# Two units' attention products in one cluster, and 17 pairs of token blocks by seven products

## The chip, the cores and the metric

One Trainium2 chip, one of its cores. The time is device microseconds for one execution of the whole program. Three runs of the kernel before gave 300.24, 300.67 and 301.27 us; the median is 300.67 us. The profile is a further execution, which took 301.17 us.

Five engines work side by side, each through its own queue in order: TensorE (PE, with its weight loads as PEld), VectorE (DVE), ScalarE (ACT), GpSimd (POOL) and SyncE (SP, which here only issues DMAs). An instruction that waits holds up everything behind it on its own engine.

## The reference, cut to what matters

Linear attention with a decay per head (retention), then a two-layer network with a tanh GELU. Eight batches, eight heads, 576 positions, head size 64:

```python
scores = scale * np.matmul(q, k.transpose(0, 1, 3, 2))
gamma = 1.0 - 2.0 ** (-5.0 - np.arange(H))
Dmat = np.where(rel >= 0, gamma[:, None, None] ** rel, 0.0)   # rel = i - j
ret = np.matmul(scores * Dmat, v)
x = ret.transpose(0, 2, 1, 3).reshape(8 * 576, 512)           # 4608 tokens
h = x @ w_in                                                  # 512 -> 2048
g = 0.5 * h * (1.0 + np.tanh(c * (h + 0.044715 * h ** 3)))
out = g @ w_out                                               # 2048 -> 512
```

## The kernel before

**Attention.** A batch's 576 positions are cut into five units: four of 128 positions and one of 64, so there are 40 units. The first four pairs of units (0 and 1, 2 and 3, 5 and 6, 7 and 8) go through "wide" code that the change leaves alone; the other 32 go one at a time. For a unit u the list of steps has: `L` (loads of q, k, v by SP), `q`, `k`, `v` (casts to fp16 with the decay, on DVE, ACT or POOL), `D` (transposes of q and k by a DMA on SP) or `t` and `y` (the same by PE and a copy), then `B,u,w` (`attend`), which is PE's part. `B` does four things: the product of unit w's queries with the running state (L498, 128 rows of the array), unit u's k-v products that go into the state (L516), unit u's scores (L526), and unit w's outputs from its masked scores (L536). The last three are 64x64 products, four to the array at once; between two groups of them PE does products on the whole 128x128 array. Behind `B`, DVE masks the scores (`m`, L651), adds the k-v products to the state (`a`, L667), and the state is copied to fp16 for the next units (`z`); ACT copies the outputs to `xT` (`x`, L555).

**Network.** The 4608 tokens are nine groups t of 512. `N,t,fc,half` is eight products of 128x256 for `h` (L708), `M,t,fc` four of 128x512 for the same amount of work; `F` and `G` are the GELUs behind them on ACT (L716). The second product, for two blocks of 128 tokens at a time (a "pair"), is done as seven half-size products in place of eight: `T` makes sums of blocks of `w_out` once (DVE, eight steps), `H` sums of blocks of g (DVE, four per pair), `W` the seven products (L809, eight instructions of 128x256 each), `V` the seven additions that assemble the result (L768 on DVE, or a copy by L241 on ACT). Fifteen pairs go this way. The four blocks of t = 0, and one block of t = 8, go by the plain product `O` (L734, four steps of four 128x512 instructions per block), and the last block by `P` (L857).

**PSUM.** There are eight banks. Two each go to `h` (pool `ps_h`), to the second product (`ps_o`), to the scores and states of `B` (`ps_s`) and to its outputs (`ps_x`). The two pools `ps_h` and `ps_o` each hand out one bank in turn; a step that takes a bank waits until the last reader of that bank has finished.

**Order.** The order of all work is one list, `ORDER`, at the head of the source. A loop at the end calls one function per step, and each step appends its instructions to its engines' queues. So the place of a step in the list sets the order on each queue, and nothing else moves it. `K` steps are products of the identity whose results nothing reads; they stand where PE waits for the first loads. SP's queue holds the loads, the DMA transposes and the stores `S` and `Q`; POOL's queue holds casts and the loads of the two weight matrices (`I`, `J`).

Of the kernel before, what the change touches and what calls it, by code (L numbers as in the profile page):

```python
# [12 lines left out]
F32 = mybir.dt.float32  # L13
F16 = mybir.dt.float16
# [3 lines left out]
Z,1,v Z,2,g L,0,0 L,0,2 q,0 L,0,1 k,0,a L,2,0 v,0,g g I,2,g I,1,g K,4 K,2 t,0,q,o K,4 K,2 X,0 a,0,1  # L18
y,0,q,a q,2 I,0,g Z,3,v t,0,k,h y,0,k,v I,3,g z,0,1,a L,2,1 a,1,1 k,2,g K,4 K,4 K,2 t,2,k,h o,1,1
Y,0,1 L,4,1 I,5,g Z,4,g m,0,1 t,2,q,o k,4,a K,4 Y,0,0 y,2,k,a y,2,q,a z,1,1,v m,0,0 K,4 R,0 t,4,k,o  # L20
Y,2,1 I,4,g L,2,2 c Z,0,g x,1 x,0 K,3 N,0,0,0 m,2,1 L,4,0 N,0,2,0 I,7,g y,4,k,v v,2,g L,5,0 F,0,0,0
I,6,g N,0,6,0 F,0,6,0 F,0,2,0 Z,5,v L,5,1 X,2 q,4 Y,2,0 K,1 t,4,q,o N,0,4,0 N,0,10,0 a,2,1 z,2,1,v
m,2,0 k,5,g F,0,4,0 N,0,8,0 J,1,g y,4,q,v a,3,1 q,5 L,5,2 F,0,10,0 R,2 J,0,g B,4,-1 z,3,1,v t,5,q,o
y,5,q,v L,7,0 x,3 N,0,12,0 F,0,8,0 x,2 J,2,g J,7,g F,0,12,0 m,4 N,0,14,0 L,4,2 J,3,g N,0,8,1 L,7,1
v,5,v F,0,14,0 F,0,8,1 t,5,k,o N,0,4,1 N,0,6,1 q,7 y,5,k,a Y,5,0 F,0,4,1 X,5 F,0,6,1 N,0,10,1 a,5,1
v,4,g t,7,q,o a,6,1 m,5,0 k,7,v J,5,g F,0,10,1 N,0,0,1 N,0,2,1 L,7,2 J,4,g F,0,0,1 y,7,q,a B,-1,4
Y,5,1 z,5,1,a N,0,12,1 t,7,k,o x,4 L,11,0 m,5,1 F,0,2,1 O,0,0 y,7,k,v J,6,g R,5 Y,7,0 O,0,4 x,5
m,7,0 L,9,0 M,1,0,0 F,0,12,1 v,7,v x,6 N,1,10,0 o,6,1 L,9,1 G,1,0,0 F,1,10,0 N,1,14,0 L,9,2 F,1,14,0
N,1,4,0 O,0,5 L,10,0 N,0,14,1 F,1,4,0 O,0,1 X,7 q,9 k,9,v T,3,1,v F,0,14,1 Y,7,1 O,0,2 N,1,8,0
F,1,8,0 N,1,12,0 O,0,6 O,0,3 M,1,0,1 e,0,0,v a,7,1 a,8,1 q,10 O,0,7 F,1,12,0 N,1,6,0 L,10,1 O,0,12  # L30
L,11,1 z,7,1,a m,7,1 O,0,13 e,0,1,a T,1,1,v D,9 O,0,8 z,8,1,g T,1,0,v G,1,0,1 F,1,6,0 z,6,1,g v,9,g
L,10,2 t,10,q,h R,7 L,12,1 y,10,q,v B,9,-1 O,0,9 T,3,0,v k,10,v m,9 x,7 t,10,k,h L,11,2 H,1,0,1,v
O,0,10 O,0,14 H,1,0,2,v L,12,2 v,10,g x,8 y,10,k,a q,11 M,1,0,2 T,2,0,v L,13,1 L,12,0 L,14,1 k,11,g
B,10,9 T,2,1,v k,12,g D,11 H,1,0,3,v N,1,6,1 a,10,0 a,10,1 G,1,0,2 v,11,g S,0,0 O,0,11 j,6,a F,1,6,1
L,19,1 m,10 N,1,12,1 T,4,0,v H,1,0,4,v F,1,12,1 k,13,g N,1,4,1 O,0,15 L,14,0 M,1,0,3 z,10,1,g
F,1,4,1 e,0,3,a q,12 x,9 T,4,1,v N,1,8,1 L,13,0 G,1,0,3 S,0,1 L,14,2 z,10,0,v j,3,a F,1,8,1 W,1,0,1
e,0,2,v L,17,1 v,14,g v,12,g B,11,10 W,1,0,6 m,11 D,12 L,15,0 V,1,0,0,a x,10 q,13 N,2,0,0 W,1,0,2
V,1,0,2,a a,11,0 D,13 V,1,0,1,v z,11,0,v a,11,1 N,1,14,1 F,2,0,0 W,1,0,7 F,1,14,1 i,0,g o,11,1
N,2,4,0 z,11,1,v B,12,11 a,12,0 N,2,8,0 m,12 F,2,4,0 k,14,v S,0,3 V,1,0,3,v z,12,0,g L,15,2 F,2,8,0
W,1,0,5 L,13,2 L,15,1 N,2,6,0 N,1,10,1 W,1,0,4 v,13,g F,2,6,0 i,1,g q,14 L,16,0 V,1,0,5,v N,2,10,0  # L40
F,1,10,1 L,16,2 N,2,2,0 L,17,0 F,2,10,0 W,1,1,1 x,11 a,12,1 V,1,0,4,v V,1,1,0,a B,13,12 W,1,0,3
L,16,1 a,13,0 q,16 q,15 V,1,0,6,v x,12 m,13 F,2,2,0 N,2,4,1 F,2,4,1 N,2,0,1 z,13,0,v F,2,0,1 a,13,1
N,2,2,1 k,15,v H,1,1,1,v H,1,1,2,v z,12,1,a k,16,v z,13,1,v M,2,12 W,1,1,2 F,2,2,1 M,2,13 v,15,g
W,1,1,6 L,19,0 D,14 D,15 H,2,0,3,v V,1,1,2,a G,2,12 B,14,13 G,2,13 N,2,8,1 H,1,1,3,v M,2,14 m,14
x,13 D,16 V,1,1,1,v L,18,1 B,15,14 F,2,8,1 H,1,1,4,v a,15,0 z,15,0,a W,1,1,7 N,2,6,1 m,15 L,18,2
x,14 a,15,1 v,16,g B,16,15 G,2,14 L,18,0 q,19 S,0,2 M,2,15 z,15,1,g V,1,1,3,v F,2,6,1 x,15 W,1,1,5
N,2,10,1 W,1,1,4 k,18,g a,16,0 a,16,1 G,2,15 F,2,10,1 H,2,0,1,v V,1,1,4,v k,17,g W,1,1,3 V,1,1,5,v
N,3,0,0 N,3,10,0 F,3,0,0 k,19,v q,18 W,2,0,1 z,16,0,g F,3,10,0 S,1,0 L,20,1 L,21,1 N,3,8,0 L,17,2
V,2,0,0,a k,20,v v,18,v D,18 N,3,4,0 o,16,1 q,17 F,3,8,0 D,17 V,1,1,6,v L,20,2 W,2,0,2 m,16
H,2,0,2,v N,3,6,0 F,3,4,0 H,2,0,4,v S,1,1 H,2,1,1,v L,23,2 L,21,0 D,19 L,24,1 L,24,0 W,2,0,6  # L50
z,16,1,g V,2,0,2,a v,17,v B,17,16 a,17,0 V,2,0,1,v z,17,0,g a,17,1 N,3,2,0 S,1,2 x,16 m,17 F,3,6,0
W,2,0,7 z,17,1,v B,18,17 x,17 L,20,0 H,2,1,3,v W,2,0,5 L,22,1 L,25,0 F,3,2,0 V,2,0,3,v m,18 a,18,0
L,21,2 N,3,14,0 z,18,0,a a,18,1 W,2,0,4 V,2,0,4,v F,3,14,0 V,2,0,5,v N,3,8,1 q,21 L,22,0 W,2,0,3
k,21,v H,2,1,2,v W,2,1,1 V,2,1,0,a F,3,8,1 B,19,18 V,2,0,6,v j,0,a N,3,4,1 W,2,1,2 W,2,1,6 V,2,1,2,a
N,3,0,1 W,2,1,7 F,3,4,1 F,3,0,1 V,2,1,1,v S,1,3 V,2,1,3,v S,2,0 L,26,0 L,19,2 q,22 q,20 N,3,14,1
D,20 H,2,1,4,v F,3,14,1 v,20,g z,18,1,v x,18 L,22,2 W,2,1,4 N,3,6,1 W,2,1,5 V,2,1,5,v F,3,6,1
N,3,12,0 D,21 W,3,0,1 V,3,0,0,a L,25,1 F,3,12,0 N,3,10,1 m,19 v,19,v L,23,1 B,20,19 V,2,1,4,v a,20,0
L,23,0 k,22,g N,3,12,1 L,29,0 L,27,0 H,3,0,1,v H,3,0,2,v W,3,0,2 F,3,12,1 F,3,10,1 W,2,1,3 k,24,g
m,20 N,3,2,1 V,3,0,2,a V,2,1,6,v v,21,g x,19 a,20,1 z,20,0,g N,4,0,0 F,3,2,1 H,3,0,4,v v,22,g
B,21,20 k,23,a N,4,6,0 D,22 F,4,0,0 W,3,0,6 q,24 k,25,v F,4,6,0 N,4,4,0 H,3,0,3,v V,3,0,1,v N,4,12,0  # L60
F,4,4,0 a,21,0 x,20 a,21,1 H,3,1,1,v v,23,v z,20,1,a o,21,1 m,21 W,3,0,5 W,3,0,7 z,21,0,a D,24
V,3,0,3,v S,2,1 F,4,12,0 N,4,2,0 B,22,21 F,4,2,0 q,23 V,3,0,4,v H,3,1,2,v x,21 W,3,0,4 q,25
V,3,0,5,v L,26,1 a,22,0 W,3,0,3 S,2,2 L,27,2 m,22 N,4,12,1 W,3,1,1 z,22,0,a D,23 L,24,2 F,4,12,1
V,3,0,6,v q,27 N,4,2,1 j,5,v L,26,2 N,4,0,1 F,4,2,1 a,22,1 z,21,1,g z,22,1,a L,25,2 B,23,22 L,28,0
V,3,1,0,a N,4,14,0 W,3,1,2 F,4,0,1 H,3,1,3,v N,4,4,1 W,3,1,6 F,4,14,0 V,3,1,1,v i,4,v S,2,3 F,4,4,1
m,23 x,22 V,3,1,2,a M,4,8 G,4,8 W,3,1,5 v,24,g L,28,1 v,25,g M,4,10 a,23,0 q,26 v,26,v G,4,10 L,27,1
N,4,14,1 W,3,1,7 a,23,1 V,3,1,3,v F,4,14,1 L,31,2 z,23,1,g M,4,9 z,23,0,a L,29,1 k,27,a B,24,23
H,3,1,4,v N,4,6,1 D,25 G,4,9 k,26,a L,29,2 M,4,11 x,23 L,28,2 W,3,1,4 F,4,6,1 V,3,1,4,v V,3,1,5,v
D,26 m,24 W,3,1,3 N,5,0,0 G,4,11 i,5,g V,3,1,6,v B,25,24 q,28 F,5,0,0 L,30,2 S,3,0 H,4,0,1,v W,4,0,1
k,28,v H,4,0,2,v x,24 S,3,3 V,4,0,0,a a,25,0 z,25,0,v N,5,2,0 W,4,0,2 F,5,2,0 m,25 N,5,6,0 D,27 D,28  # L70
a,25,1 B,26,25 N,5,14,0 H,4,0,4,v v,28,g S,3,1 L,30,0 v,27,v F,5,6,0 V,4,0,2,a N,5,8,0 x,25 F,5,14,0
W,4,0,6 H,4,0,3,v F,5,8,0 a,26,0 a,26,1 V,4,0,1,v v,29,g z,25,1,g L,32,0 N,5,10,0 z,26,0,v W,4,0,7
L,31,1 N,5,4,0 V,4,0,3,v H,4,1,1,v W,4,0,4 m,26 F,5,10,0 H,4,1,2,v B,27,26 x,26 W,4,0,5 L,32,2
V,4,0,5,v F,5,4,0 N,5,10,1 o,26,1 N,5,4,1 q,29 F,5,10,1 V,4,0,4,v m,27 W,4,1,1 V,4,1,0,a L,30,1
N,5,12,0 S,3,2 a,27,0 L,35,0 W,4,0,3 q,30 H,4,1,3,v V,4,0,6,v k,30,v H,4,1,4,v F,5,12,0 W,4,1,2
j,7,g W,4,1,6 F,5,4,1 z,26,1,a N,5,6,1 z,27,0,g k,29,g a,27,1 N,5,14,1 V,4,1,2,a H,5,0,1,v L,31,0
q,31 V,4,1,1,v L,36,2 D,30 W,4,1,7 V,4,1,3,v k,31,a B,28,27 F,5,6,1 F,5,14,1 a,28,0 W,4,1,5 S,4,1
H,5,0,2,v N,5,12,1 a,28,1 D,29 V,4,1,4,v z,28,0,a x,27 v,31,g z,28,1,v z,27,1,g N,5,0,1 F,5,12,1
W,4,1,4 L,34,0 N,5,8,1 L,33,1 F,5,8,1 m,28 F,5,0,1 B,29,28 m,29 v,30,g i,7,a V,4,1,5,v W,4,1,3
N,5,2,1 x,28 B,30,29 L,34,1 F,5,2,1 H,5,0,4,v x,29 a,30,0 V,4,1,6,v W,5,0,1 m,30 H,5,0,3,v V,5,0,0,a  # L80
H,5,1,3,v v,32,v a,30,1 S,4,0 N,6,0,0 z,30,0,g L,33,0 W,5,0,2 q,33 W,5,0,6 V,5,0,2,a N,6,12,0
V,5,0,1,v W,5,0,7 D,31 B,31,30 F,6,0,0 k,34,a L,34,2 x,30 q,32 V,5,0,3,v H,5,1,1,v W,5,0,5 M,6,8
L,36,0 q,34 a,31,0 L,32,1 k,33,v L,33,2 F,6,12,0 W,5,0,4 H,5,1,2,v G,6,8 N,6,2,0 i,6,a m,31
V,5,0,5,v F,6,2,0 M,6,9 q,35 W,5,1,1 G,6,9 M,6,4 G,6,4 L,35,1 V,5,0,4,v L,38,1 N,6,2,1 S,4,2 S,5,1
z,30,1,g k,32,v L,39,2 F,6,2,1 D,32 W,5,0,3 M,6,5 a,31,1 V,5,1,0,a z,31,0,a j,4,a G,6,5 W,5,1,2
V,5,0,6,v M,6,11 B,32,31 v,33,g o,31,1 V,5,1,2,a W,5,1,7 M,6,6 G,6,11 S,5,0 S,4,3 a,32,0 G,6,6 x,31
z,32,0,a D,33 W,5,1,6 m,32 v,34,g V,5,1,1,v M,6,7 M,6,10 a,32,1 z,31,1,v j,1,a V,5,1,3,v z,32,1,a
B,33,32 L,37,1 a,33,0 W,5,1,4 L,36,1 G,6,7 N,6,0,1 k,36,a G,6,10 k,35,g z,33,0,a F,6,0,1 L,37,0
# [856 lines left out]
```

## Time and profile before

| what | value |
|---|---|
| three runs | 300.24, 300.67, 301.27 us |
| profiled execution | 301.17 us, of which the span from first to last instruction is 299.1 us |
| TensorE's granted clock | 1.00 over the span |
| steps of PE in the list | 34 `B`, 124 `N`, 20 `M`, 105 `W`, 20 `O`, 12 `t`, 11 `K` |
| DMA | 49.51 MB, mean 166 GB/s |

The page gives busy time per engine, forty equal slices of the span in tenths, the chain of work that ended last, and groups of instructions by line. "Mean ns of one" of a matmul is its own length from start to end; matmuls overlap, so what one costs the kernel is the distance between two starts. That distance can be read from the chain, whose pieces give the time that a run of so many instructions took.

### The profile page before, as it was taken

The page shows a single profiled execution, that of the slowest core. Times are in us where ns is not written, and L with a number is a line of the kernel's source. Part 1 is how long each engine was busy: PE and PEld are TensorE (multiplying, and loading weights), DVE is VectorE, ACT ScalarE, POOL GpSimd, SP SyncE. Part 2 cuts the span into 40 slices and gives each one's busy share as a digit, 9 for nine tenths or more (in the row PEclk, how much of TensorE's full clock was granted, in tenths as well). Part 3 has the DMA queues.
Part 4 walks back from the last instruction along what each step waited for, and adds up shares of the span by engine and source line. Part 5 has one row for each costly group of instructions (what it writes and reads, how often), then busy time and mean ns, then how long its engine had stood idle before and what let it go on. Part 6 is the DMA issues. An engine that isn't in the chain of part 4 may idle for free.

```text
span 299.1 us, 9534 instructions
## 1 busy us (share of the span) xinstructions
PE 286.2 (96%) x4086; PEld 234.9 (79%) x4086; DVE 185.2 (62%) x408; ACT 144.5 (48%) x282; POOL 80.7 (27%) x125
## 2 busy tenths in 40 slices
PE   3898999999999999989999999999999999999995
PEld 1466777668887788878887888887788888888874
DVE  8566663599629687357835877777288274643310
ACT  2463663436346544335577445444584546433321
POOL 5980810391321312113121125134041130200000
PEclk9999999999999999999999999999999999999999
DMA  6999999937999987999997995897995507100303
GB/s 191 279 230 239 283 197 202 214 75 161 189 212 155 237 125 184 206 221 189 221 226 158 241 234 119 168 182 167 215 180 112 122 21 142 37 2 0 144 18 125
DMA packets 135370, 49.51 MB, mean 166 GB/s; under 512 B 117152, under 2 KB 129824, under 8 KB 135328
## 3 DMA queue, kind: packets, MB, share of 16 engines
q1 hardware_dynamic: 130976, 44.71, 67.8%
q0 software_dynamic: 4352, 4.20, 8.4%
q8 instruction: 32, 0.52, 0.8%
q14 instruction: 10, 0.08, 0.1%
HBM read 36.70 MB, written 9.44 MB: 154 GB/s over the span
## 4 chain that ended last, share of the span: by engine, by line
PE 79%; DMA 6%; POOL 6%; DVE 4%; SPq 2%; issue 1%; ACT 1%; ACTq 0%; POOLq 0%; DVEq 0%
PE hps L708 37%; PE ops L809 27%; PE ops L734 6%; DMA w_in_sb<-in_moe_w_in_dram 3%; PE sk L516 2%; PE x L498 2%; POOL w_in_sb L212 2%; DMA pages<-in_q_dram 2%; DMA pages<-in_v_dram 2%; PE sk L526 1%; POOL wide L407 1%; PE x L536 1%; SPq L189 1%; PE ops L857 1%; POOL v L392 1%
## 5 line engine op out<-in xcount | busy, mean ns | idle before, releaser
L708 PE MATMUL hps<-xT,w_in_sb 128*128 128x256 f16 (+2 forms) x1120 | 143.4, 276 | 1.5 <-DMA w_in_sb<-in_moe_w_in_dram 1.5
L716 ACT ACTIVATE gT<-hps 128x512 f16<-128x512 f32 x144 | 84.8, 597 | 79.3 <-PE hps L708 79.0
L708 PEld LDWEIGHTS <-w_in_sb 128*128 128x128 f16 x1120 | 105.4, 98 | 20.7 <-DMA w_in_sb<-in_moe_w_in_dram 2.5
L809 PEld LDWEIGHTS <-ssum 128*128 128x128 f16 x480 | 46.1, 98 | 7.4 <-issue 0.6
L809 PE MATMUL ops<-tsum,ssum 128*128 128x256 f16 x360 | 46.1, 273 | 0.0
L809 PEld LDWEIGHTS <-gT 128*128 128x128 f16 x360 | 34.6, 98 | 6.8 <-issue 1.5
L392 POOL TENSOR_TENSOR v<-pages,dec 128x512 f16<-128x512 f32 (+1 forms) x24 | 23.8, 1001 | 51.9 <-DMA pages<-in_v_dram 38.0
L768 DVE TENSOR_TENSOR ost<-u,ops 128x256 f32<-128x256 f32 x45 | 18.5, 417 | 27.0 <-PE ops L809 25.4
L809 PE MATMUL ops<-w_out_sb,gT 128*128 128x256 f16 x240 | 31.2, 273 | 1.4 <-DVE ost L768 1.4
L768 DVE TENSOR_TENSOR u<-u,ops 128x256 f32<-128x256 f32 x30 | 12.5, 418 | 29.6 <-PE ops L809 19.9
L243 POOL CAST sz<-s 64x256 f16<-64x256 f32 x26 | 14.7, 564 | 55.4 <-DVE s L667 37.9
L392 DVE TENSOR_TENSOR qk<-pages,dec 128x512 f16<-128x512 f32 (+1 forms) x32 | 22.1, 696 | 10.0 <-DMA pages<-in_q_dram 10.0
L768 DVE TENSOR_TENSOR ssum<-gT,ssum 128x1024 f16<-128x1024 f16 x30 | 22.7, 758 | 0.2
L768 DVE TENSOR_TENSOR ssum<-gT 128x1024 f16<-128x1024 f16 x30 | 21.8, 732 | 0.8 <-ACT gT L716 0.8
L555 ACT ACTIVATE xT<-x 128x512 f16<-128x512 f32 (+1 forms) x26 | 14.4, 563 | 13.8 <-PE x L536 13.7
L651 DVE TENSOR_TENSOR ret<-sk,mask 128x512 f16<-128x512 f32 (+1 forms) x32 | 19.8, 618 | 1.4 <-PE sk L526 1.4
L734 PE MATMUL ops<-w_out_sb,gT 128*128 128x512 f16 x80 | 19.6, 379 | 0.0
L241 ACT CAST sz<-s 64x256 f16<-64x256 f32 x36 | 14.5, 402 | 8.8 <-DVE s L667 6.8
L685 POOL TENSOR_TENSOR sz<-s,gend 64x256 f16<-64x256 f32 x8 | 7.7, 959 | 36.9 <-DVE s L667 22.6
L667 DVE TENSOR_TENSOR s<-s,sk 128x256 f32<-128x256 f32 x36 | 15.0, 416 | 4.2 <-PE sk L526 3.6
L241 ACT COPY ost<-ops 128x256 f32<-128x256 f32 (+2 forms) x20 | 7.9, 394 | 18.0 <-PE ops L809 9.9
L809 PE MATMUL ops<-w_out_sb,ssum 128*128 128x256 f16 x120 | 15.6, 273 | 0.5 <-DVE ost L768 0.5
(96 smaller groups left out, 273.5 us busy)
## 6 DMA issues: line engine op xcount, KB each, us to landing
out_dram<-ost SPq DMA_DIRECT2D x35, 256.0 KB, 3.2
pages<-in_q_dram SPq DMA_DIRECT2D x32, 256.0 KB, 5.0
pages<-in_k_dram SPq DMA_DIRECT2D x24, 256.0 KB, 4.8
pages<-in_v_dram SPq DMA_DIRECT2D x24, 256.0 KB, 4.4
pages<-in_v_dram SPq DMA_DIRECT2D x4, 512.0 KB, 7.5
pages<-in_k_dram SPq DMA_DIRECT2D x4, 512.0 KB, 6.9
w_in_sb<-in_moe_w_in_dram POOLq DMA_DIRECT2D x8, 256.0 KB, 10.0
w_out_sb<-in_moe_w_out_dram POOLq DMA_DIRECT2D x8, 256.0 KB, 10.6
```

The source lines that it names most:

```text
L241: nc.scalar.copy(out=o, in_=i)
L243: (nc.vector if eng == "v" else nc.gpsimd).tensor_copy(out=o, in_=i)
L392: eng.tensor_tensor(out=out, in0=s["raw"][:, i, 0:n], in1=dec[:, i // 2, s["j"], 0:n].unsqueeze(2).to_broadcast([128, n, D]), op=ALU.mult,)
L555: nc.scalar.activation(out=xT[:, :, o : o + G * (b - a)].rearrange("c p (h s) -> c p h s", s=G), in_=x[:, a:b].rearrange("c h p s -> c p h ...
L651: nc.vector.tensor_tensor(out=ret[:, :, 0:n], in0=now["sk"][:, :, 0, 0:n], in1=mask.unsqueeze(1).unsqueeze(1).to_broadcast([128, 2, n, G]) ...
L667: nc.vector.tensor_tensor(out=s32, in0=state[0], in1=kv, op=ALU.add)
L685: (nc.vector if eng == "v" else nc.gpsimd).tensor_tensor(out=z[o : o + 64, :, hl, :], in0=s32[o : o + 64], in1=gend[o : o + 64], op=ALU.mult,)
L708: nc.tensor.matmul(hps[:, i, :], w_in_sb[:, ct, 128 * (fc + i) : 128 * (fc + i) + 128], xT[:, ct, TB * t % XR + lo : TB * t % XR + hi], st ...
L716: nc.scalar.activation(out=gTs[t][:, fc : fc + TB // (hi - lo), lo:hi], in_=h.pop((t, fc, lo)), func=AF.Gelu_apprx_tanh, bias=0.0, scale=1.0,)
L734: nc.tensor.matmul(ops[t, tcc], gTs[t][:, ft, 128 * tcc : 128 * tcc + 128], w_out_sb[:, ft, :], start=(ft == 0), stop=(ft == NFC - 1),)
L768: (nc.vector if eng == "v" else nc.gpsimd).tensor_tensor(out=out, in0=a, in1=b, op=op)
L809: nc.tensor.matmul(p["ps", bank][:, HN * col : HN * col + HN], a[:, k], b[:, k], start=(k == 0 and i in (1, 6)), stop=(k == HK - 1), skip_ ...
```

## The change

The step `C,u,u2,w,w2,pool` is new. It calls `attend` with two units u and u2 for the k-v products and scores and two units w and w2 for the outputs. In PE's order: the products of w and of w2 with the state, then k-v products and scores of u, then those of u2, then the outputs of w and w2. The outputs of both lie in the two banks of `ps_x`. The scores and k-v products of u lie in `ps_s` as before; those of u2 take both banks of `pool`, which is `h` or `o`. For that the two pools become one tile of two banks each, handed out by `take`, in the same turn as before.

Of the 34 `B` steps 5 remain, and there are 15 `C` steps. Eleven of them name pool `h`, four name `o`.

The four blocks of t = 0 become two pairs, so 17 pairs go by seven products. `O` goes from 20 steps to 4, `W` and `V` from 105 to 119 each, `H` from 60 to 68. Of the eight `T` steps, which all stood before the first product of t = 1's first pair, six now stand before the first product of t = 0's first pair and two between its third and its last.

The list is made anew. `N` goes from 124 to 92 steps and `M` from 20 to 52 (4 of them in quarters in both); `t` and `y` go from 12 to 18 each and `D` from 30 to 27: q and k of units 9, 12, 21 and 24 are transposed by PE and unit 10's by a DMA. `K` steps go from 34 products to 39. Among the casts `k` moves from 9 on ACT, 12 on POOL, 15 on DVE to 12, 14, 10; `z` from 20, 20, 16 to 17, 23, 16; `V` has 85 steps on DVE in place of 75. At the start the first load is k of unit 0, then q of units 0 and 2, then v of 0 and 2; POOL's first weight load stands before the first cast of v; `w`, which makes ACT load its GELU table, is the second step and was the last. The last attention step `B,-1,39` stands earlier: more of the network's products come behind it.

```diff
-B,10,9 T,2,1,v k,12,g D,11 H,1,0,3,v N,1,6,1 a,10,0 a,10,1 ...
+z,10,0,a F,1,4,1 i,6,a F,1,6,0 B,9,-1 W,0,1,2 L,16,1 V,0,1,1,v m,9 L,15,0 L,13,0 C,11,12,9,10,h
...
+    banks = {
+        "h": ps_h.tile([128, 2, 512], F32, name="banks_h"),
+        "o": ps_o.tile([128, 2, 512], F32, name="banks_o"),
+    }
+    turn = {"h": 0, "o": 0}
+
+    def take(pool):
+        turn[pool] += 1
+        return banks[pool][:, turn[pool] % 2]
...
-    def attend(u, ux):
-        now, last = st.get(u), st.get(ux)
-        if last:
-            c, m = last["c"], last["np"]
-            x = ps_x.tile([128, 2, 2, HP, G], F32, tag="x", name="x")[:, :, 0]
-            last["x"] = x
-            first = {}
+    def attend(us, ws, pool=None):
+        us, ws = [u for u in us if u >= 0], [st[w] for w in ws if w >= 0]
+        if ws:
+            tile_x = ps_x.tile([128, 2, 2, HP, G], F32, tag="x", name="x")
+        first = {}
+        for e, last in enumerate(ws):
+            c, m, u = last["c"], last["np"], last["u"]
+            last["x"] = x = tile_x[:, :, e]
...
-        if now:
-            n = now["np"]
-            kT, qT = now["kT"], now["qT"]
-            sk = ps_s.tile([128, 2, 2, HP, G], F32, tag="s", name="sk")
+        for e, u in enumerate(us):
+            now = st[u]
+            n, kT, qT = now["np"], now["kT"], now["qT"]
+            if e:
+                take(pool), take(pool)
+                sk = banks[pool].rearrange("c i (a p s) -> c i a p s", a=2, p=HP)
+            else:
+                sk = ps_s.tile([128, 2, 2, HP, G], F32, tag="s", name="sk")
...
-        h[t, fc, lo] = hps = ps_h.tile([128, TB // n, n], F32, tag="h", name="hps")
+        h[t, fc, lo] = hps = take("h").rearrange("c (i n) -> c i n", n=n)
...
-            ops[t, tcc] = ps_o.tile([128, DM], F32, tag="o", name="ops")
+            ops[t, tcc] = take("o")
...
-        "B": lambda u, ux: attend(None if u < 0 else u, None if ux < 0 else ux),
+        "B": lambda u, w: attend([u], [w]),
+        "C": lambda u, u2, w, w2, pool: attend([u, u2], [w, w2], pool),
```

## The prediction

> **What bounds the kernel now.** I read the page's busy times first, then the slices, then the chain.
>
> ```profile
> span 299.1 us, 9534 instructions
> ...
> PE 286.2 (96%) x4086; PEld 234.9 (79%) x4086; DVE 185.2 (62%) x408; ACT 144.5 (48%) x282; POOL 80.7 (27%) x125
> ...
> PE   3898999999999999989999999999999999999995
> ...
> DVE  8566663599629687357835877777288274643310
> ...
> PE 79%; DMA 6%; POOL 6%; DVE 4%; SPq 2%; issue 1%; ACT 1%; ACTq 0%; POOLq 0%; DVEq 0%
> ```
>
> PE's slices are full from the fifth on. The other engines' shares of the chain lie mostly in the first 30 us and in a few stalls. So behind the start, the time is what PE issues plus what it waits. The waits of PE alone say how little that is:
>
> ```profile
> PE busy L873 <- DVE ident L338: 4.5, 1, 4.5
> PE ops L809 <- DVE ost L768: 1.8, 2, 1.4
> PE hps L708 <- DMA w_in_sb<-in_moe_w_in_dram: 1.5, 3, 0.7
> PE x L580 <- ACT wide L241: 0.7, 1, 0.7
> PE sk L516 <- POOL v L392: 0.4, 1, 0.4
> ```
>
> Only the second and fifth lie behind the start. The larger of the two waits for DVE (1.4 us, at 132.4) is a late load: DVE stood 1.81 us before a cast of q whose load had not landed, until 129.01, and the addition that frees the bank was queued behind it.
>
> Prices next. The chain in order of time gives what runs of products cost:
>
> ```profile
> 183.10 2.62 PE ops L809 x24
> 216.47 1.73 PE hps L708 x8
> 289.95 2.59 PE ops L734 x12
> ```
>
> A 128x256 product takes 2.62/24 = 0.109 us, a 128x512 one 1.73/8 = 0.216 (2.59/12 agrees). And the timeline of PE around one `B`:
>
> ```profile
> 152.17 0.40 PE L498 MATMUL x<-qkT,sz 128*128 128x64 f16 x8
> 152.50 0.32 PE L516 MATMUL sk<-v,qk 64*64 64x64 f16 x16
> 152.65 0.30 PE L526 MATMUL sk<-qkT 64*64 64x64 f16 x16
> 152.77 0.30 PE L536 MATMUL x<-ret,v 64*64 64x64 f16 x16
> 153.01 0.50 PE L708 MATMUL hps<-xT,w_in_sb 128*128 128x256 f16 x3
> ```
>
> Eight L498 products cover 0.40 us and one lasts 0.193 (its group's mean), so they start (0.40 - 0.193)/7 = 0.030 apart: eight are 0.24 us, but L516 starts 0.33 behind. Going into the 64x64 products costs 0.09. Sixteen of them take 0.12 to 0.15; the last sixteen take 0.24 to the next large product. Coming out costs 0.12. A cluster costs 0.21 us over its work.
>
> **The change part by part.**
>
> *Pairs.* Two pairs lose 2 x 32 products of 128x512 (13.8 us) and get 2 x 56 of 128x256 (12.2 us): -1.6 us on PE.
>
> *N to M.* 32 times, eight products of 0.109 (0.872) become four of 0.216 (0.864): -0.3.
>
> Against both stands a rule of the Trainium skill (TensorE: Matmul & The Clock Gate, Back-to-back issue gap): in a real stream a 512-wide product costs about 131 ns, and the 216 is that of an isolated one. Here whole streams keep 216, so the trace does not agree. By the rule these two parts together (64 more 512-wide, 144 fewer 256-wide) would give 64 x 0.131 - 15.7 = -7.3 in place of -1.9; that is a rival below.
>
> *Clusters.* 34 `B` become 5 `B` and 15 `C`. Some stand next to other 64x64 steps (`X`, `Y`, `R`) and share a cluster; counted along the two lists there are 43 clusters before and 31 after. 12 x 0.21 = -2.5.
>
> *Transposes.* Sixteen more by PE. Eight `tp` products take 0.45 us in the timeline (37.05 to 37.50): +0.9. DMA loses three transposes on SP's queue, which bounds nothing there.
>
> PE's own sum is -3.5 us.
>
> *The start.* Before, real work of the network begins at 20.29. v of unit 0 was the load behind q; now k and q of unit 2 stand before it too, 1 MB more. At the first 10 us' 227 GB/s it lands 4.6 us later, by 12.9 at worst in place of 8.3, and POOL's cast of it (1.9 us) also has two weight-load issues of 0.70 each (four took 2.79) before it. `X,0` moves from 10.6 to about 14.8; behind it two additions (0.42 each) and a mask (1.2) give 17.3, under the 18.4 that held `R,0` before. `t,5,q` however now stands ahead of `R,0`, and q of unit 5 is the seventh load: 3.7 MB with some 1 MB of `w_in` between, 20 us, and a cast of 1.2. (`g`, eight memsets or 1.3 us, moves ahead of the first cast of q on DVE; that ends at 8.5 and not 7.3, still under the fifteen `K` products that now stand before `t,0,q`.) `N` would begin at about 22.8 with 0.8 us more work already done: +1.7 at worst. At best the waits for `w_in` go (1.5, its first loads being issued earlier) and the GELU table's load (1.28 on ACT at 20.26, for which PE waited 0.2): -1.7. The five more `K` products, 1.1 us, fill waits of this stage. I take +0.2.
>
> *Sums of w_out.* Eight `T` of 0.78 come before t = 0's first pair. The last load of `w_out` was issued at 37.6 and takes 10.6 to land. POOL's work before that issue in the new list comes to some 25 us from 7.7 on, so 33 to 38; landed by 44 to 49. The third product, the first that needs them, stands 26.4 us of PE's work behind the first `N`, so at 47 to 49. Up to 2 us if both are at their bad ends; I take nothing, since the middle values (46.5 and 48) leave room for the two `T` in front of that product that read the last load.
>
> *Banks held.* No row of before shows this. `C` needs both banks of a pool: the last GELU of 0.6 has at least one step (0.87) and `C`'s own first part (0.8) to end in, so going in is free unless ACT is late. Coming out, the next `N` or `W` of that pool waits until DVE has read u2's scores and states. For each `C` I added DVE's steps in the list up to the last such read (a = 0.42, m = 0.68 or 0.42, H = 0.75, V = 0.42, z = 0.6, o = 0.44, k = 0.51) and PE's up to the next taker. `C,31,32`: DVE 5.0, PE 3.5. `C,11,12`: 4.4 against 3.5. `C,25,26`, `C,27,28`, `C,37,38`: 3.5 against 2.6. `C,33,34`, `C,35,36`, `C,17,18`: PE has the more. Eleven are short, by 6.8 us in all. That is the upper end, if DVE starts only when `C` ends. It need not: u's states are done 0.6 us before (u2's group and the outputs come behind them), which leaves 2.1, and `H` and `V` at the front of six need nothing of `C`. Below: 0. I take +0.8, near the lower end, because DVE has an idle share to run ahead in.
>
> *DVE and the loads.* DVE gets eight `H` (6.0), ten `V` (4.2), five `y` (2.1), one `v` (0.7), loses five `k` (2.6) and one `e` (0.7): +9.7 us. It lies beside PE's work:
>
> ```profile
> 40.00:130.00 90.00, 89.24 (x1308) 72.09 (x1307) 59.78 (x115) 43.18 (x85) 24.57 (x33) 1.00 0.91 183
> 130.00:230.00 100.00, 98.63 (x1512) 83.33 (x1511) 70.55 (x144) 54.76 (x112) 25.15 (x31) 1.00 0.89 188
> ```
>
> (Columns: stretch, length, busy PE, PEld, DVE, ACT, POOL, clock, DMA share, GB/s.) DVE is 66% and 71% busy there; with the 9.7, and with the last attention step 38.0 us of PE's work before the end where it stood 27.5, it comes to about 78%. DMA is at 0.90; the last load stands some 7 us of PE's work earlier, 0.93. Both still fit, and ACT (-0.3) and POOL (+4) do too. I take nothing here, and the same few stalls as before; if the cover is gone, each late load costs PE about 1.4 us, the row at 132.4.
>
> *Sum.* -1.6 - 0.3 - 2.5 + 0.9 + 0.2 + 0.8 = -2.5. The profiled execution took 301.17 us (2.07 around its span), which is 0.5 over the median of 300.67. It would take 298.7; on the median's scale 298.2.
>
> **Rivals.** 0.3%, 0.9 us, is about what a measurement of this kernel tells from no change.
>
> A, slower: the held banks become a wait of PE behind every short `C`, all 6.8 us of it: 300.67 - 3.5 + 0.2 + 6.8 = 304.2. It decides from a mean of (3.5 - 0.2)/15 = 0.22 us per `C`. For it: DVE is in order and busier. Against: DVE's idle shares, and the waits on DVE before were two. A page speaks for it: the Trainium skill (Perfetto Trace Analysis, Optimization Strategy) reads a gap that recurs on the engine that should be full as too little PSUM for the next tile; no row of before shows one.
>
> B, no change: late loads. A denser DVE and DMA turn two stalls of the 132.4 kind into four: +2.8, 301.0. For it: DMA share 0.90 to 0.93. Against: three fewer DMA transposes.
>
> C, more: the start's waits for `w_in` go and the holds cost nothing: 300.67 - 3.5 - 1.5 = 295.7.
>
> D, wide products that overlap more than 0.216 apart allows: with the rule's 131 ns, 300.67 - 7.3 - 2.5 + 0.9 + 0.2 + 0.8 = 292.8. Every stream in the chain speaks against it, so it gets no chance.
>
> **How the numbers follow.** Forecast 0.59 (own range 296.7 to 299.7), A 0.13, B 0.13, C 0.15, D 0. Faster 0.59 + 0.15 = 0.74, same 0.13, slower 0.13. The range goes from under C, 294.8, to 302.0, which takes in B and the beginning of A.
>
> **What would show it.** Clusters: the starts behind L516, L526 and L536 groups, 31 times about 0.21. Pairs: 952 products of L809, 16 of L734, at 0.109 and 0.216. Holds: PE waiting on DVE at L651 or L667 right behind a `C`; over 3 us in all makes me wrong. Start: the first L708 between 19 and 23 us. Loads: PE waiting on L768 behind a DVE cast that waited for a load.

## The result and the profile after

The changed kernel takes 380.50 us (median of four runs, 376.42 to 382.73); the kernel before, run beside it, takes 300.46. The ratio is 1.263, with a 95% interval from 1.251 to 1.275. The prediction said 298.2 us, within 294.8 to 302.0, and gave a slower kernel 13 chances in 100. It was wrong by 82 us and in its sign. The profiled execution took 382.73 us, with a span of 381.0. Ratios in this text are of mean times and leave out a run more than 1.5% above the fastest of its kernel, as the profiled one is here (its mean granted clock was 0.982; that of the fastest, 376.42 us, was 0.995).

From the page of the changed kernel, engines, slices and the share of the chain:

```profile
span 381.0 us, 9471 instructions
...
PE 302.8 (79%) x4027; PEld 230.7 (61%) x4027; DVE 194.2 (51%) x427; ACT 141.0 (37%) x280; POOL 79.4 (21%) x132
...
PE   5866867877788968778887779879788878988776
...
PE 54%; ACT 10%; DVE 4%; issue 3%; ACTq 0%; DVEq 0%
```

PE has fewer instructions than before (4027 for 4086), and its work by the number of products is about 1 us less. But hardly a slice is full now: 79% in place of 96%. The loss is not in one place; it is spread over the whole span. ACT, which was 1% of the chain, is 10%, although it is busy for 3.5 us less than before. So an engine that has little to do has come onto the path, because PE stops for it again and again. The waits of PE alone (engine, its tile and line, what it waited for, and then us in all, how often, the longest):

```profile
PE banks_h L726 <- ACT gT L734: 42.3, 53, 2.3
PE banks_o L829 <- DVE ost L786: 5.3, 9, 0.9
PE banks_o L829 <- DVE u L786: 4.9, 7, 1.5
PE banks_h L892 <- DVE ident L340: 4.5, 1, 4.5
PE banks_o L829 <- ACT ost L243: 2.4, 5, 0.6
```

L726 is `N` and `M`, L734 the GELU, L829 `W`, L786 the additions `V`. Before, the waits of PE had no row for a GELU. Now 53 wait, 0.8 us each. A wait is counted from the end of the last product; undisturbed, the next step begins 0.17 us before that end (its eight products are issued in 0.87 us, but end after 1.04). So the 53 cost about 53 x 0.97 = 51 us. One of them in the timeline of the changed kernel, with PE's and ACT's lines (start, length, and in brackets the idle time before and what ended it):

```profile
338.50 1.04 PE L726 MATMUL banks_h<-xT,w_in_sb 128*128 128x256 f16 x8
...
339.57 0.60 ACT L734 ACTIVATE gT<-banks_h 128x512 f16<-128x512 f32 x1 [1.15 <-PE banks_h L726]
...
340.22 1.03 PE L726 MATMUL banks_h<-xT,w_in_sb 128*128 128x256 f16 x8 [0.68 <-ACT gT L734]
...
341.09 1.04 PE L829 MATMUL banks_o<-w_out_sb,gT 128*128 128x256 f16 x8
```

These are `N,8,10,0` and `N,8,14,0`, which follow each other on PE. Eight products are issued in 0.87 us. The second step begins 1.72 us behind the first: when the first step's products have ended (1.04), ACT reads the bank (0.60), and only then does PE go on. The second step writes the other bank. It had no reason to wait for the reader of the first.

It works the other way too. A GELU that stands in the list behind the next step's products waits for these as well:

```profile
96.39 1.91 PE L726 MATMUL banks_h<-xT,w_in_sb 128*128 128x256 f16 x16 [0.69 <-ACT gT L734]
...
98.33 0.60 ACT L734 ACTIVATE gT<-banks_h 128x512 f16<-128x512 f32 x1 [2.00 <-PE banks_h L726]
...
98.98 1.03 PE L726 MATMUL banks_h<-xT,w_in_sb 128*128 128x256 f16 x8 [0.69 <-ACT gT L734]
```

The first row is two steps, `N,1,14,1` and `N,2,0,0`. The GELU is that of the first, whose products end at about 97.4; it starts when those of the second have ended (98.30). The list has 66 such GELUs. None of them starts before the later products have ended, and the median one starts 1.75 us behind its own; in `split`, the first experiment below, that is 0.04.

To see all of this loss, I laid every step of PE's list on the trace: the distance from its first product to the next step's first, less the number of its products times their spacing (0.109 us for a 128x256 product, 0.216 for a 128x512 one, 0.056 for a transpose, 0.030 for the products with the state, 0.0075 for a 64x64 one). What is left over is lost. Before that is 20.4 us in all, in the changed kernel 102.0. In front of `N` and `M` it grew from 6.0 to 55.5, in front of `W` from 6.5 to 27.7. The `C` steps are not where it is: what stands in front of them comes to 1.5 us, and the waits of PE have no row for DVE's reads of u2's scores and states in `banks_h` or `banks_o`. A part of the loss is a lower clock: the granted clock is 0.50 in four stretches of 3.4 us, from 63.3, 206.7, 309.1 and 360.3 us on. Estimated from these lengths, that is at most 6.8 of the 82 us.

### The profile page after: what moved, and what is told of

Its sections match the earlier page's. It is cut to its first block, busy times and chain, and to the rows that moved or that the text cites. A ratio compares the mean times of both kernels' runs of the same rounds, so it can differ in the third digit from the quotient of the medians.

```text
span 381.0 us, 9471 instructions
## 1 busy us (share of the span) xinstructions
PE 302.8 (79%) x4027; PEld 230.7 (61%) x4027; DVE 194.2 (51%) x427; ACT 141.0 (37%) x280; POOL 79.4 (21%) x132
## 4 chain that ended last, share of the span: by engine, by line
PE 54%; ACT 10%; DVE 4%; issue 3%; ACTq 0%; DVEq 0%
PE banks_h L726 25%; PE banks_o L829 23%; ACT gT L734 8%; DVE ost L786 2%; PE x L511 1%; PE banks_o L752 1%; DVE u L786 1%; ACT ost L243 1%; DVE s L685 1%; PE x L554 1%; PE sk L533 1%; ACT sz L243 1%; PE banks_h L876 1%; PE sk L543 0%; PE banks_o L876 0%
## 5 line engine op out<-in xcount | busy, mean ns | idle before, releaser
L726 PE MATMUL banks_h<-xT,w_in_sb 128*128 128x256 f16 (+2 forms) x992 | 146.7, 294 | 42.3 <-ACT gT L734 42.3
L726 PEld LDWEIGHTS <-w_in_sb 128*128 128x128 f16 x992 | 94.8, 99 | 76.9 <-issue 51.9
L734 ACT ACTIVATE gT<-banks_h 128x512 f16<-128x512 f32 x144 | 82.3, 597 | 152.4 <-PE banks_h L726 148.2
L829 PEld LDWEIGHTS <-ssum 128*128 128x128 f16 x544 | 52.8, 98 | 23.9 <-issue 11.8
L829 PE MATMUL banks_o<-tsum,ssum 128*128 128x256 f16 x408 | 53.0, 275 | 9.3 <-DVE u L786 3.7
L786 DVE TENSOR_TENSOR u<-u,banks_o 128x256 f32<-128x256 f32 x34 | 14.3, 419 | 71.0 <-PE banks_o L829 60.5
L786 DVE TENSOR_TENSOR ost<-u,banks_o 128x256 f32<-128x256 f32 x51 | 21.0, 419 | 54.8 <-PE banks_o L829 44.2
L829 PEld LDWEIGHTS <-gT 128*128 128x128 f16 x408 | 40.1, 100 | 14.2 <-issue 6.5
L829 PE MATMUL banks_o<-w_out_sb,gT 128*128 128x256 f16 x272 | 37.0, 281 | 3.4 <-DVE ost L786 2.8
L786 DVE TENSOR_TENSOR ssum<-gT 128x1024 f16<-128x1024 f16 x34 | 23.9, 707 | 14.5 <-ACT gT L734 14.4
L786 DVE TENSOR_TENSOR ssum<-gT,ssum 128x1024 f16<-128x1024 f16 x34 | 23.8, 699 | 0.2
L829 PE MATMUL banks_o<-tsum,gT 128*128 128x256 f16 x136 | 17.6, 272 | 1.6 <-DVE ost L786 0.9
L829 PE MATMUL banks_o<-w_out_sb,ssum 128*128 128x256 f16 x136 | 17.6, 273 | 1.5 <-DVE ost L786 1.0
L892 PE MATMUL banks_h<-ident 128*128 128x512 f16 x39 | 11.3, 442 | 6.3 <-DVE ident L340 4.5
```

The source lines that it names most:

```text
L726: nc.tensor.matmul(hps[:, i, :], w_in_sb[:, ct, 128 * (fc + i) : 128 * (fc + i) + 128], xT[:, ct, TB * t % XR + lo : TB * t % XR + hi], st ...
L734: nc.scalar.activation(out=gTs[t][:, fc : fc + TB // (hi - lo), lo:hi], in_=h.pop((t, fc, lo)), func=AF.Gelu_apprx_tanh, bias=0.0, scale=1.0,)
L786: (nc.vector if eng == "v" else nc.gpsimd).tensor_tensor(out=out, in0=a, in1=b, op=op)
L829: nc.tensor.matmul(p["ps", bank][:, HN * col : HN * col + HN], a[:, k], b[:, k], start=(k == 0 and i in (1, 6)), stop=(k == HK - 1), skip_ ...
L892: nc.tensor.matmul(t, ident, ident.unsqueeze(1).to_broadcast([128, 4, 128]), start=True, stop=True, skip_group_check=True,)
```

## The experiments

**Theory.** The two banks of `h`, and the two of `o`, were two tiles of a pool before and are one tile of two banks now. A step that takes one bank of such a tile waits for every reader of the tile that stands ahead of it in the list, whichever bank it reads; and a reader waits for every step that writes the tile ahead of it. The order in which the banks are handed out is the same, but the two no longer work as two buffers. **Rivals.** The list itself is bad (loads, order, a full DVE), or the `C` steps hold both banks for long, as the prediction's rival A had it.

**Each bank a tile of its own.** `split` undoes this one thing in the changed kernel. The list and the clusters stay as they are; only u2's mask becomes two instructions of DVE, one for each bank.

```diff
-    ps_h = ctx.enter_context(tc.tile_pool(name="ps_h", bufs=1, ...))
-    ps_o = ctx.enter_context(tc.tile_pool(name="ps_o", bufs=1, ...))
+    ps_h = ctx.enter_context(tc.tile_pool(name="ps_h", bufs=2, ...))
+    ps_o = ctx.enter_context(tc.tile_pool(name="ps_o", bufs=2, ...))
...
     def take(pool):
-        turn[pool] += 1
-        return banks[pool][:, turn[pool] % 2]
+        p = ps_h if pool == "h" else ps_o
+        return p.tile([128, 512], F32, tag=pool, name="bank_" + pool)
...
-                sk = banks[pool].rearrange("c i (a p s) -> c i a p s", a=2, p=HP)
+                sk = [take(pool).rearrange("c (a p s) -> c a p s", a=2, p=HP) for _ in range(2)]
...
```

> The changed kernel with one edit: each of the four banks of the pools h and o is a tile of its own again; u2's scores and states lie in two such tiles, so its mask is two DVE instructions of 0.42 us in place of one of 0.68. List and clusters stay. Theory 1 (a tile of two banks is waited for as one, so every N waits for the GELU just before it): the 0.85 us behind most N and M go, and the time falls from 380 to 295 to 301 us, 298 in the middle. Theory 2 (the new list or the held banks are what costs): it stays above 360. Theory 3 (both): between 310 and 350.

Measured: 300.21 us (299.02 to 304.14), ratio 0.9973 (0.9945 to 1.0001) to the kernel before at 301.44. From its page, and its waits of PE:

```profile
PE 284.0 (96%) x4027; PEld 228.0 (77%) x4027; DVE 201.3 (68%) x441; ACT 143.2 (48%) x280; POOL 80.7 (27%) x132
...
PE   3976999999999999999999999999999999999995
```

```profile
PE bank_h L893 <- DVE ident L340: 4.5, 1, 4.5
PE bank_o L469 <- ACT wide L243: 3.4, 2, 2.7
PE x L592 <- ACT xT L560: 1.0, 1, 1.0
PE bank_o L469 <- DVE qk L400: 0.6, 1, 0.6
PE bank_o L469 <- DVE ost L787: 0.6, 1, 0.6
```

Eighty microseconds come back with the same list, the same clusters and the same products. Every wait for a GELU is gone, and the slices behind the start are full. No wait of PE behind a `C` shows either. That settles both rivals: neither the list nor the holds of `C` is the cause.

**The same thing done to the kernel before.** Three kernels take the old list and the old `B` steps, and make only the pool of `h`, only that of `o`, or both into one tile of two banks.

```diff
-    ps_h = ctx.enter_context(tc.tile_pool(name="ps_h", bufs=2, ...))
+    ps_h = ctx.enter_context(tc.tile_pool(name="ps_h", bufs=1, ...))
...
+    banks["h"] = ps_h.tile([128, 2, 512], F32, name="banks_h")
...
-        h[t, fc, lo] = hps = ps_h.tile([128, TB // n, n], F32, tag="h", name="hps")
+        h[t, fc, lo] = hps = take("h").rearrange("c (i n) -> c i n", n=n)
...
```

> The kernel before, with its own list and its single B steps; only the two pools h and o become one tile of two banks each, handed out in the same turn. Theory 1: 350 to 385 us, since its list too has many N close behind each other. Theory 2: 300 to 302 us, nothing changes. Theory 3: 320 to 350.

> The kernel before, only pool h as one tile of two banks. Theory 1: some 55 waits of up to 0.85 us for a GELU, 335 to 350 us. Theory 2: 300 to 302 us.

> The kernel before, only pool o as one tile of two banks. Theory 1: W waits for additions of both banks; the changed kernel's waits of PE on DVE and ACT at the second product suggest 310 to 330 us. Theory 2: 300 to 302 us.

Measured, with the kernel before at 301.44 us:

| kernel | us | ratio, 95% |
|---|---|---|
| `one_tile_both` | 354.45 | 1.178 (1.174 to 1.181) |
| `one_tile_h` | 340.95 | 1.131 (1.129 to 1.134) |
| `one_tile_o` | 319.26 | 1.060 (1.057 to 1.063) |

The waits of PE that cost most in `one_tile_h`, and two rows of `one_tile_o`:

```profile
PE banks_h L718 <- ACT gT L726: 28.4, 45, 1.7
```

```profile
PE banks_o L819 <- DVE ost L778: 6.9, 10, 1.2
PE banks_o L819 <- DVE u L778: 2.7, 5, 0.9
```

So the slow-down needs nothing of the clusters, the pairs or the new list. The two pools alone cost 39.5 and 17.8 us; both together cost 53.0 and not 57.3, since some waits of the one hide in waits of the other: in front of `W`, the accounting by steps has 20.2 us with `o` alone and 16.3 with both.

**Which pool costs what in the changed kernel.** `split` with one of the two pools made one tile again:

```diff
+    both = ps_h.tile([128, 2, 512], F32, name="banks_h")
+    turn = [0]
...
     def take(pool):
-        p = ps_h if pool == "h" else ps_o
-        return p.tile([128, 512], F32, tag=pool, name="bank_" + pool)
+        if pool == "o":
+            return ps_o.tile([128, 512], F32, tag=pool, name="bank_" + pool)
+        turn[0] += 1
+        return both[:, turn[0] % 2]
```

> split, but the pool of N and M (h) is one tile of two banks again, as in the changed kernel; o's banks keep their own tiles. Theory (a step that takes one bank of the tile waits for the reader of the other): of the 83.6 us that the changed kernel loses over split in front of PE's steps, 52.3 stand before N and M: about 300.2 + 52 = 352, and PE waits on ACT's GELU in front of some 55 N and M. Rival (only u2's scores and states, which span both banks in that tile, hold the pool): 9 of 15 C take h, at most 2 us each: under 318.

> split, but the pool of W, O and t (o) is one tile of two banks again; h's banks keep their own tiles. Theory: 23.4 us before W, 1.3 before O and 1.5 before t are what the changed kernel loses there over split: about 300.2 + 26 = 326. Rival (u2's six holds of o alone): under 312. If the two parts, this run's and that with h, add to less than the 80 us of both, waits of the one pool hide in those of the other.

Measured: 351.80 us with `h` as one tile, 329.23 with `o`. Over `split` that is 51.6 and 29.0, together 80.6, where the changed kernel stands 80.3 over `split`. The waits of PE in `split_but_h`:

```profile
PE banks_h L732 <- ACT gT L740: 41.4, 53, 1.6
PE banks_h L898 <- DVE ident L340: 4.5, 1, 4.5
PE bank_o L474 <- DVE qk L405: 2.7, 2, 1.6
```

These are again 53 waits, as in the changed kernel. The accounting by steps had said 52 and 26. Of the 3 us that it missed for `o`, 1.2 are the wait for k of unit 5 at the start, 3.9 us long in that profile and 2.7 in `split`'s; behind it PE works for 5.6 us at a granted clock of 0.50, in `split` for 3.4, which by an estimate from these lengths is about 1 us more. (Of the fifteen `C`, eleven put u2 into `h` and three into `o`, and one has no u2; what was expected counted nine and six.)

**What a cluster costs.** `split` gains only 0.3% over the kernel before. Its parts can still be tested. `cluster_cut` puts the whole-array products of w2 between the 64x64 products of u and those of u2, so that each `C` goes into 64x64 products twice. The products are the same.

```diff
-        for e, last in enumerate(ws):
+        def older(e, last):
...
+        if ws:
+            older(0, ws[0])
         for e, u in enumerate(us):
...
+            if not e and len(ws) > 1:
+                older(1, ws[1])
```

> split with each C cut in two: the products of w2's old state, of 128 rows, stand between u's 64x64 products and u2's, not in front of both. Same products, 15 more changes into 64x64 products and out of them. If a change in and out costs the 0.21 us that the prediction read from one B (0.26 by split's own mean over 20 steps), 15 of them cost 3.1 to 3.9 us: 303.3 to 304.1. If what B's cost is something else (the short products' own issue, or the wait for the first operands), nothing: 300.2.

Measured: 304.36 us, ratio 1.0087 (1.0051 to 1.0123), against `split`'s 0.9973: 3.4 us more by the ratios, 4.2 by the medians, just over what was expected. But the times of either kernel spread over 4 to 5 us, so the price is better read from the traces. In its profile the `B` and `C` steps take 8.08 us more than their products, in `split`'s 5.16. The difference is 2.92 us for 15 changes, 0.195 us each; it lies in the `C` steps alone, and every one of the 15 grows, by 0.15 to 0.23 us. (The rest of this profile's 6.2 us over `split`'s span lies elsewhere: the wait for k of unit 5 at the start is 2.2 us longer in it, and one transpose at 64 us waits 1 us for a cast.) So the price of 0.21 us that the prediction read from one `B` is that of a change in and out.

**The start.** Where is the rest of `split`'s expected gain? Its accounting by steps shows it: PE has lost 10.5 us by 33 us, where the kernel before had lost 8.1, and its `K` products come on top (8.4 us for 7.3). PE's timeline of `split`:

```profile
27.77 0.82 PE L469 MATMUL bank_o<-ident,wide 128*128 128x128 f16 x8 [2.75 <-ACT wide L243]
28.38 1.06 PE L638 MATMUL x<-qkT,sz 128*128 128x128 f16 x8
29.37 1.07 PE L650 MATMUL x<-xT,wide 64*64 64x128 f16 x32
30.37 1.57 PE L727 MATMUL bank_h<-xT,w_in_sb 128*128 128x128 f16 x16
31.86 0.42 PE L609 MATMUL sk<-qkT 64*64 64x128 f16 x16
```

and its windows of 2 us (stretch, length, busy PE, PEld, DVE, ACT, POOL, granted clock, DMA share, GB/s):

```profile
26.00:28.00 2.00, 0.23 (x4) 0.24 (x5) 0.00 (x0) 1.33 (x2) 0.00 (x0) 1.00 1.18 223
28.00:30.00 2.00, 2.00 (x39) 1.80 (x40) 0.89 (x2) 0.69 (x2) 0.00 (x0) 0.51 1.15 309
30.00:32.00 2.00, 2.00 (x44) 1.73 (x36) 0.50 (x1) 0.03 (x1) 1.39 (x1) 0.64 1.13 294
```

`t,5,k` transposes k of unit 5. ACT casts it, and its 512 KB land late. PE stands 2.75 us; behind that its granted clock is 0.51 and 0.64 for four microseconds, and the same steps take longer than in the next kernel (the group L638 1.06 us in place of 0.61). `start_mended` lets ACT do three more GELUs before this cast and moves work of the network in front of `t,5,k`.

```diff
-y,5,q,a z,1,1,v t,4,k,o L,7,0 F,0,4,0 k,5,a Y,2,1 a,2,1 z,2,1,v N,0,0,0 I,4,g N,0,2,0 a,3,1 L,7,1
-t,5,k,o F,0,0,0 m,2,1 R,2 y,5,k,v y,4,k,v L,4,2 M,0,12,0 F,0,2,0 I,5,g q,4 Y,5,0 t,4,q,o G,0,12,0
...
+y,5,q,a z,1,1,v t,4,k,o L,7,0 F,0,4,0 Y,2,1 a,2,1 z,2,1,v N,0,0,0 I,4,g F,0,0,0 N,0,2,0 a,3,1 L,7,1
+m,2,1 y,4,k,v R,2 F,0,2,0 x,3 N,0,6,0 x,2 L,4,2 I,5,g F,0,6,0 k,5,a N,0,4,1 F,0,4,1 t,5,k,o y,5,k,v
+q,4 M,0,12,0 G,0,12,0 Y,5,0 t,4,q,o N,0,6,1 F,0,6,1 M,0,12,1 v,5,g q,7 J,1,g G,0,12,1 X,5 M,0,12,2
...
```

> The changed kernel with each bank a tile of its own, as in split, with one stretch of the list mended: k of unit 5, whose load lands last, is cast on ACT behind the GELUs of N,0,0,0 and N,0,2,0 and not in front of them; t,5,k and Y,5,0 come later, N,0,6,0, N,0,4,1 and N,0,6,1 earlier. Theory (the start is what eats the gain): in split's profile PE stands 2.75 us before t,5,k (25.0 to 27.8), and its granted clock is 0.51 and 0.64 in the four us behind it, which costs about 1.9 us more. With the stall gone both go: 3 to 4.5 us under split's 300.2, so 295.5 to 297.5, a ratio of 0.98 to 0.99 to the kernel before; first N stays at about 21.7. Rival (DMA sets the pace there, and the stall only moves to the next product that needs a late load): 299.5 to 300.5, with a wait of PE of over 2 us elsewhere before 45 us.

Measured: 299.60 us, ratio 0.9953 (0.9933 to 0.9973). The rival was nearer. In its waits of PE the stall has moved, as the rival said it would:

```profile
PE bank_o L469 <- DVE qk L400: 2.1, 1, 2.1
PE bank_o L469 <- ACT wide L243: 1.8, 2, 1.3
```

`t,4,q` now waits 2.1 us for the cast of q of unit 4, which comes by the next of the late loads, and the clock in this execution is 0.63 in the two microseconds behind it. `start_filled` therefore brings still more of the network forward, work that needs no load which is still on its way:

```diff
-q,4 M,0,12,0 G,0,12,0 Y,5,0 t,4,q,o N,0,6,1 F,0,6,1 M,0,12,1 ...
+... N,0,4,1 F,0,4,1 k,5,a N,0,0,1 F,0,0,1
+N,0,6,1 F,0,6,1 t,5,k,o y,5,k,v N,0,2,1 F,0,2,1 q,4 M,0,12,0 G,0,12,0 Y,5,0 M,0,12,1 G,0,12,1 t,4,q,o
...
```

> start_mended, with the work of the network that needs no late load brought forward: N,0,6,0, N,0,4,1, N,0,0,1, N,0,6,1 and N,0,2,1 and two M stand in front of t,4,q, four of these N in front of t,5,k; N,0,0,1 and N,0,2,1 leave later places for it. If PE only ran out of work while the loads of units 4 and 5 were on their way, its waits between 20 and 38 us, about 5 us in start_mended's profile (1.0, 0.2, 0.5, 2.05 and some 1.2 at a granted clock of 0.63), fall under 2 and the clock stays at 1.00: 296.5 to 298, a ratio of 0.985 to 0.990. If the loads set the end of the whole start and not only of these steps, the wait comes back at a later load (X,5, t,7,q) and the time stays at 299 to 300.

Measured: 298.84 us, against 300.57 for the kernel before on the same chip: ratio 0.9934 (0.9912 to 0.9957). PE's timeline has these groups with an idle time before them from 20 to 38 us:

```profile
20.00 0.62 PE L470 MATMUL bank_h<-ident,wide 128*128 128x128 f16 x8 [0.38 <-DVE wide L416]
...
22.61 0.45 PE L593 MATMUL x<-wide,wide 64*64 64x64 f16 x32 [0.97 <-ACT xT L561]
...
28.55 2.78 PE L728 MATMUL bank_h<-xT,w_in_sb 128*128 128x256 f16 x24 [0.21 <-ACT xT L561]
...
36.99 0.42 PE L610 MATMUL sk<-qkT 64*64 64x128 f16 x16 [0.53 <-DVE xT L618]
```

Both long stalls are gone, and the clock is 1.00 in every window from 20 to 38 us. The time is 0.8 us over the upper end of what was expected: the gain at the start comes back as shorter losses later (the longest 0.9 us at 42 and 0.8 at 53, not far from where the two steps that were moved forward had stood). In this profile PE's last product ends at 294.2 us, in `split`'s at 294.1; but that execution of `split` (299.06 us) was among its shortest, and this one (299.36) among the longest of `start_filled`. So the traces show that the stalls are gone, and the gain itself rests on the times alone. By these, this is the version that beats both kernels, by 0.7% and some 21%.

## Why the prediction was wrong, step by step

**The step that failed is one that the prediction does not have.** It goes through pairs, clusters, transposes, start, sums, holds and loads, but the line of the diff that makes each of the two pools one tile of two banks is in none of them. I took it to be a renaming ("handed out by `take`, in the same turn as before") and so costed it at nothing without naming what covers it. The part that comes closest, *Banks held* (+0.8, with ends 0 and 6.8), asks only who waits behind a `C`. It should have asked who waits for whom in all 144 `N` and `M` and all 119 `W`, now that both banks have one name. The runs put +80 us there: 51.6 for `h` and 29.0 for `o`.

It could have been priced from what was known, if roughly. Eight products last 1.04 us, a GELU 0.60; in one buffer the next step can begin 1.72 us behind the last, not 0.87, which costs 0.85. Along the new list, 77 of the 144 `N` and `M` have the GELU of the `N` or `M` just before them ahead of them in the list, and in 24 of these no other work of PE lies between. Work that lies between can cover the wait. So the estimate runs from 24 x 0.85 = 20 us to 77 x 0.85 = 65 us, where 51.6 was measured. It is wide, and it leaves out the GELUs that wait for later products, but even its lower end would have turned the forecast from faster to slower.

**Rival A.** Its time (304.2) and its place (behind the short `C`, for DVE) were wrong. `split` has not one wait behind a `C`, although it holds the same banks for u2. What the prediction cited beside it fits the changed kernel better than its own use of it: the Trainium skill (Perfetto Trace Analysis, Optimization Strategy) reads the same gap, repeated on the engine that should be full, as too little PSUM for the next tile. The trace has the repeated gap, 53 waits of 0.8 us, but not for want of banks: there were as many as before, and two banks that are waited for as one are one buffer.

**The rest of the sum** can be judged in `split`, which has all of the change but the merged tiles. By steps on the trace:

| term | forecast, us | in `split`, us |
|---|---|---|
| pairs, `N` to `M`, transposes: PE's products | -1.0 | -1.0 |
| clusters | -2.5 | -3.05 |
| the start with its `K` products | +0.2 | +3.4 |
| holds and stalls behind the start | +0.8 | -1.4 |
| sum | -2.5 | -2.05 |

The sum is PE's last end, 294.1 us for 296.1; the profiled execution took 299.06 us for 301.17, and the medians differ by 1.2. The count of L809's products is as foretold, 952 (the page has them as 544 and 408, by their weights), and so are their spacings.

*Clusters*: the price was right, 0.195 by `cluster_cut`.

*The start* was mis-sized. I looked at what moves the first `N` and gave it +1.7 at worst; it did begin 1.4 us later (21.66 for 20.29 us), between the 19 and 23 us that I had named. I did not look behind the first `N`, at the loads of unit 5 that now come before the network has enough work, and I did not see that a stall there also lowers the clock.

*Sums of w_out*: no wait of a `W` for a `T` shows in `split`. *Holds*: none. *DVE and the loads*: DVE's busy time grew by 16 us and not 9.7 (the mask of u2 takes two instructions in `split`, which is part of it), and it stays hidden at 68%. One stall of the kind that I had read at 132.4 is left (0.7 us at 123, before `t,21,q`).

So had the banks kept their own tiles, the change would be worth 0.3% as its list stands (the interval includes 1.0), and 0.7% with the start put in order.

## What to carry to other kernels

What makes two buffers out of two banks is not the banks, but that they are waited for separately: before two buffers are put into one tile so that one instruction can reach both, ask of every user of either, all along the list, which reader of the other stands ahead of it, and of every reader, which later writer does; price the first at the reader's time plus the 0.17 us or so by which the last product's end lies behind the next one's turn. When a diff is costed part by part, a line that only renames or re-allocates is a part as well, and its price is zero only if the waits it makes are the same. And when work is moved in front of late loads, look behind the first product of the main work too: a stall of 2 to 3 us there can cost half as much again in clock (1.5 us behind 2.75 in `split`).

## What the runs showed of the hardware that I had not expected

**Idle time lowers the clock for microseconds.** In `split` a wait of 2.75 us is followed by four microseconds at 0.51 and 0.64, which is 0.50 for 3.4 of them. In `start_mended` the same steps ran at 1.00:

```profile
25.66 0.61 PE L638 MATMUL x<-qkT,sz 128*128 128x128 f16 x8
26.20 0.64 PE L650 MATMUL x<-xT,wide 64*64 64x128 f16 x32
26.77 1.05 PE L727 MATMUL bank_h<-xT,w_in_sb 128*128 128x256 f16 x8
...
29.55 0.62 PE L469 MATMUL bank_o<-ident,wide 128*128 128x128 f16 x8 [0.50 <-ACT wide L243]
30.01 1.06 PE L727 MATMUL bank_h<-xT,w_in_sb 128*128 128x128 f16 x16
31.00 0.42 PE L609 MATMUL sk<-qkT 64*64 64x128 f16 x16
```

From start to start, `R,2` (L638 and L650) took 1.99 us in `split` for 1.11 here, the transposes (L469) 0.61 for 0.46, and the first quarter of `M` 1.50 for 0.99: 1.5 us on top of the wait. Not every such wait is followed by a lower clock: in `split_but_o` PE stands for 2.28 us until 134.8, and the clock stays at 1.00.

The eleven traces of this case show what decides it. In each, the stretches at 0.50 begin a whole number of steps of 3.41 us apart (in the changed kernel 42, 30 and 15 steps). With all traces cut into such steps, and PE's idle time counted in each, every step at 1.00 in which PE stood for 2.0 us or more is followed by one at 0.50 (seven of them, 2.01 to 2.75 us). None with less than 1.75 us is, and of the six between, three are. The 2.28 us of `split_but_o` fall across two steps, 1.46 us into the first and 0.8 into the second. Short waits that add up do the same: two of the four stretches in the changed kernel come behind steps with 1.91 and 1.86 us of idle time, in waits of at most 1.2 us.

The Trainium skill (TensorE: Matmul & The Clock Gate, Part 1: The HAM clock gate) states that the array falls to half its clock after an idle window of about 3.4 us. The traces agree with the half (0.50), and the 3.4 us are the length of a step; but PE was not idle for the whole of any step that was followed by 0.50, and in `start_mended` 2.05 us of idle time were enough.

**The merged tile guards more than the memory asks for.** The Trainium skill (PSUM — Partial Sum Buffer, PSUM bank collisions raise a hardware error) gives as its rule that PSUM be guarded by semaphores per bank and quadrant. `split` guards by bank and the changed kernel by two banks together; that difference is the 80 us measured here.
